# Cutting five mebibytes of zero stores into parts that load the DMA engines unevenly

## The chip, the cores and the metric

The kernel runs on one core of a Trainium2 chip. The metric is the device time of one execution in microseconds (us). Of the kernel before there are three runs, 450.79, 450.80 and 451.68 us, with a median of 450.8 us. All times and lines come from one further execution under the profiler.

## The reference

The reference is the forward pass and the gradient of a small decoder that handles one token. Two layers, A (attention) and B (a feed-forward layer), are applied twice with the same weights:

```python
x = x + A(layernorm(x)); x = x + B(layernorm(x))
x = x + A(layernorm(x)); x = x + B(layernorm(x))

# A: 32 query heads over 4 key/value heads, only the last W = 4096 of 32768 cached positions
q = x @ wq;  p = softmax(q k^T / sqrt(128));  out = (p v) @ wo
# B: h = x @ w1 + b1;  act = h * tanh(softplus(h));  out = act @ w2

out, vjp = jax.vjp(f, x, k_cache, v_cache, wq, wo, w1, b1, w2)
return out, *vjp(grad_out)
```

All is bfloat16, D = 1024, 32 x 128 = 4096 attention columns, F = 3584. The gradients of the two caches have the caches' own size, 4 x 32768 x 128 each. The positions outside of the window of 4096 get no gradient, so 28672 of 32768 rows of each head are zeros, which the kernel must write: 7 MiB for each of 8 (cache, head) pairs, 56 MiB in all. The weights' gradients are outer products of rank 2 (one row from each application of the layer), some 30 MiB, and the windows of the caches' gradients are 8 MiB.

## The kernel before, in words

The order of all work is written out by hand; nothing is rescheduled. A forward part (two A and two B layers) is followed by a backward part in reverse order, and that by a tail which forms the outer products on TensorE, evacuates them with VectorE and ScalarE (`evac`, L306 and L309) and stores them.

**Loads.** SyncE (SP in the profile) issues the weights as 1 MiB pieces into a ring of 8 slots (`Ring`, issue at L71). A piece is asked for in a fixed order and issued once a slot is free. SP issues the stores of the tail too (L1025 and L1030). Each DMA counts on one of a few semaphores that are used in turn, so an issue also waits until the DMA that used the semaphore before has landed.

**Zeros.** `zt` is a tile of 128 partitions x 4096 columns of zeros, 8 KiB per partition. The 56 MiB of zeros are cut into 56 pieces (`zjobs`), each of 128 rows of 8 KiB. GpSimd (POOL) issues them: `zeros(n, after)` at L257 first copies one element of `after` into a scratch tile (L260), which makes Pool wait until `after` has been computed, and then issues n pieces (L265). The calls are strewn over the second half of the kernel at places chosen by hand. Eight semaphores serve these DMAs in turn. The first piece is issued at 114.7 us and the last at 334.7 us of the span.

**The place of the change.** It lies at the start of the backward pass of the second B layer. `dh1` is the gradient at the activation's input, made from `da1` and the activation's derivative `mp1` (L975), and `zeros(8, dh1)` (L977) follows on Pool's queue. Then comes `dn_b1` (L836), which transposes W1 block by block on TensorE (L474), evacuates the blocks and multiplies them with `dh1` (L493), with no load in it since W1 is resident. Its result `g3` gates `zeros(4, g3)` (L981). `attn_bwd` follows, whose weights come through the ring again.

**Around the end.** `dn1` calls `twins` (L1041), which issues four copies of two rows each that spread the outer products' factors over other partitions (L1043); `take_back` (L819) issues copies of two times 8, 28 or 32 rows of 256 B for the same purpose, `rowize` (L1015) and `rowize_f` (L861) copies of 7 to 32 rows. With them ready, `unit_dw` (L1051) and `units_kv` (L1102) fill one 128 x 1024 block after another. The stores' buffers are the ring's slots, the places of the K and V windows and of W1.

Of the kernel before, what the change touches and what calls it, by code (L numbers as in the profile page):

```python
# [15 lines left out]
P = 128  # L16
# [5 lines left out]
G = 4  # L22
# [71 lines left out]
def kernel(  # L94
# [22 lines left out]
    nc = tc.nc  # L117
# [13 lines left out]
    def sb(shape, dtype, name):  # L131
        return keep.tile(shape, dtype, name=name)
# [24 lines left out]
    ZC = 4096  # L157
    zt = sb([P, ZC], BF16, "zt")
# [36 lines left out]
    for hi in range(4):  # L195
        r = slice(32 * hi, 32 * hi + 32)
# [46 lines left out]
            ring.want(("2", k, c), w2_v[:, c], [P, 4, D], own)  # L243


    zjobs = []
    for out_t in (out_2, out_3):
        for g in range(G):
            dst = out_t[0, g, 0:ZR, :].rearrange("(p r) d -> p (r d)", p=P).rearrange("p (r c) -> p r c", c=ZC)
            for k in range(dst.shape[1]):  # L250
                zjobs.append(dst[:, k, :])
    zjobs.reverse()

# [3 lines left out]
    def zeros(n, after=None):  # L257

        if after is not None and zjobs:
            nc.gpsimd.tensor_copy(pz[0:1, pz_n[0] % 16:pz_n[0] % 16 + 1], after[0:1, 0:1])  # L260
            pz_n[0] += 1
        for _ in range(n):
            if zjobs:
                dst = zjobs.pop()
                nc.gpsimd.dma_start(dst, zt[:])  # L265


    KEEP_Q = (5, 6, 7)
# [519 lines left out]
    def last_da(k):  # L788

        for c in (5, 6):  # L790
            if k == 0:
                da_dots(c)
            else:
                ring.release(("2", 0, c))
        if k:
            nc.gpsimd.memset(zt[:], 0.0)
            zeros(1)

    def wo_hook1(c):
        if c == 0:  # L800
            zeros(7, OC[:, 0, 1:2])
        if c:
            conv(1)
# [18 lines left out]
    put_by("OC", OC, HQ)  # L822
    put_by("NA", NA, TD)
    zeros(8, x3)
    sB1 = mlp_fwd(1, x3, st3, lambda: conv(1, "A"))
    put_by("NB", NB, TD)
# [4 lines left out]
    dh1 = sb([P, TF], FP32, "dh1")  # L831
# [4 lines left out]
    def dn_b1(g):  # L836

        bcast(lambda c: DHC[:, c, 1:2], STAY)
        mv_open()
        even()  # L840
        for t in range(TD):
            rowdot(W1[:, t, 0:STAY * P], [LB[0][:, 0:512]], 512, dnp[:, t:t + 1], True)
            for k in range(3):
                f0, n = STAY + 8 * k, 8
                w = W1[:, t, f0 * P:(f0 + n) * P]
                turned(w, n, lambda w=w, f0=f0, n=n, t=t, k=k: mv(w, n, TP[:, t:t + 1], lambda i: DHC[:, f0 + i, 1:2], k == 2),
                       None, f_block)
        flush()
        conv(3, "A")
        return ln_bwd(dnp, sB1["n32"], sB1["rstd"], g, "B1", lambda k: conv(k, "A"))  # L850
# [123 lines left out]

    nc.vector.tensor_tensor(out=dh1[:], in0=da1[:, 0:TF], in1=mp1[:], op=ALU.mult)  # L975
    nc.vector.tensor_copy(DHC[:, :, 1], dh1[:])
    zeros(8, dh1)  # L977
    g3 = dn_b1(g4)
    sB1["act_late"]()
    put_by("AC", AC, TF)  # L980
# [272 lines left out]
```

## Time and profile before

| | before |
|---|---|
| runs, median of 3 | 450.8 us (450.79 to 451.68) |
| profiled execution | 450.36 us, span 448.6 us |
| bytes moved by DMA | 181.40 MB, of it 58.72 MB on Pool's queue (zeros) and 121.84 MB on SP's |
| HBM | 81.84 MB read, 98.62 MB written |
| TensorE busy | 313.9 us (70%), granted clock 0.673 |
| VectorE busy | 261.2 us (58%) |
| ScalarE busy | 210.0 us (47%) |
| GpSimd busy | 38.9 us (9%), of it 29.7 us in 56 issues of zeros, 0.53 us each |
| zero piece, issue to landing | 8.5 us least, 20.5 median, 41.1 most |

How to read it: the span is the time from the first to the last instruction, and the run's time has some 1.8 us more around it. The DMA share in windows is the mean over the core's sixteen DMA engines, so one engine alone counts as 0.06; a share of 1.01 to 1.02 means that records overlap a little and that all sixteen are busy. A DMA of 128 rows is spread over the sixteen engines with 8 rows each, and it has landed when all sixteen have reported. The chain of work is followed back from the last instruction, each step to what released it.

### The profile page before, as it was taken

What the parts mean: (1) busy time and instruction counts of PE and PEld (TensorE: products, weight loads), DVE (VectorE), ACT (ScalarE), POOL (GpSimd) and SP (SyncE); (2) the same over time, 40 slices, a digit from 0 to 9 for tenths busy, and PEclk for the clock granted to TensorE, in tenths of its full rate; (3) what the DMA queues carried; (4) which work ended last, traced back from release to release, by engine and by line L of the source; (5) the groups of instructions that cost most, each with busy time, mean ns of one, the idle gap of its engine ahead of it and who ended that gap; (6) DMA issues with size and microseconds to landing.
All of it is one profiled execution on the core that took longest, in us unless ns stands there. A gap on an engine that the chain in (4) does not pass through costs nothing.

```text
span 448.6 us, 12825 instructions
## 1 busy us (share of the span) xinstructions
PE 313.9 (70%) x5681; PEld 239.7 (53%) x5681; DVE 261.2 (58%) x516; ACT 210.0 (47%) x242; POOL 38.9 (9%) x86
## 2 busy tenths in 40 slices
PE   3845542465699797986988666797966988899600
PEld 3735532455586686986986545787941222235300
DVE  4504746367551664864477447663566999998600
ACT  2501101011058576870474441570647999999600
POOL 1000000001222212102101001012130000000000
PEclk9955555556559899995798657986765555555555
DMA  8999999979999999999999999999999999999993
GB/s 336 420 420 418 421 420 418 418 312 427 393 421 422 422 420 415 398 420 423 424 423 422 427 423 419 424 393 422 424 406 415 400 417 419 417 421 408 377 408 143
DMA packets 28085, 181.40 MB, mean 404 GB/s; under 512 B 3674, under 2 KB 3702, under 8 KB 9590
## 3 DMA queue, kind: packets, MB, share of 16 engines
q1 hardware_dynamic: 19874, 121.84, 66.1%
q0 software_dynamic: 8064, 58.72, 31.5%
q8 instruction: 44, 0.72, 0.6%
q14 instruction: 11, 0.09, 0.1%
q10 hardware_dynamic: 92, 0.02, 0.0%
HBM read 81.84 MB, written 98.62 MB: 402 GB/s over the span
## 4 chain that ended last, share of the span: by engine, by line
DMA 53%; PE 22%; ACT 7%; DVE 7%; issue 4%; SPq 1%; ACTq 0%; DVEq 0%
DMA ring<-in_B_w_dram 13%; DMA W<-in_A_wo_dram 8%; PE BIG L474 8%; DMA ring<-in_A_wq_dram 7%; DMA ring<-in_A_wo_dram 5%; DMA W<-in_A_wq_dram 5%; ACT ring L309 4%; DMA out_dram<-W 4%; DMA W<-in_B_w_dram 4%; PE TP L493 3%; DMA W<-dr_AC 2%; DMA W<-in_A_k_cache_dram 2%; PE wide L1051 2%; DVE KT L306 2%; PE SC L347 2%
## 5 line engine op out<-in xcount | busy, mean ns | idle before, releaser
L309 ACT COPY ring<-BIG 128x1024 bf16<-128x1024 bf16 x52 | 51.5, 1014 | 49.3 <-PE BIG L474 45.0
L1051 PE MATMUL wide<-W 2*128 2x512 bf16 x232 | 51.7, 597 | 10.7 <-ACT ring L309 1.7
L474 PE MATMUL BIG<-ident_bf,ring 128*128 128x128 bf16 x672 | 54.3, 233 | 1.8 <-issue 1.0
L474 PEld LDWEIGHTS <-ring 128*128 128x128 bf16 x768 | 52.0, 108 | 3.4 <-issue 2.6
L451 DVE CUSTOM_DVE_ANT_0 junk<-ring,SC 128x1024 bf16<-128x1024 bf16 x32 | 38.9, 1215 | 11.6 <-DMA ring<-in_B_w_dram 11.2
L1051 PEld LDWEIGHTS <-W 2*128 2x128 bf16 x240 | 12.6, 102 | 48.1 <-issue 43.7
L493 PEld LDWEIGHTS <-ring 128*128 128x128 bf16 x864 | 29.9, 98 | 10.0 <-issue 5.8
L309 ACT CAST ring<-wide 128x1024 bf16<-128x1024 f32 x35 | 33.9, 1040 | 2.0 <-PE wide L1051 0.9
L265 POOL DMA_DIRECT2D out_dram<-zt x56 | 29.7, 534 | 50.3 <-DMA out_dram<-zt 49.3
L306 DVE CAST ring<-wide 128x1024 bf16<-128x1024 f32 (+1 forms) x29 | 32.3, 1145 | 2.5 <-PE wide L1102 1.2
L309 ACT COPY KT<-BIG 128x1024 bf16<-128x1024 bf16 x22 | 21.6, 1007 | 21.4 <-PE BIG L652 19.5
L451 DVE CUSTOM_DVE_ANT_0 junk<-ring,DSX 128x1024 bf16<-128x1024 bf16 x24 | 29.4, 1224 | 0.8
L306 DVE COPY ring<-BIG 128x1024 bf16<-128x1024 bf16 x32 | 21.8, 689 | 12.8 <-PE BIG L474 10.2
L474 PE MATMUL BIG<-ident_bf,W 128*128 128x128 bf16 x280 | 23.8, 235 | 3.4 <-DMA W<-in_A_wo_dram 2.5
L309 ACT COPY W<-BIG 128x1024 bf16<-128x1024 bf16 x20 | 20.0, 1015 | 10.0 <-PE BIG L474 9.8
L536 PE MATMUL MV<-NA,ring 128*128 128x1 bf16 x512 | 15.3, 165 | 13.2 <-DMA ring<-in_A_wq_dram 11.7
L536 PEld LDWEIGHTS <-ring 128*128 128x128 bf16 x512 | 14.7, 104 | 14.0 <-DMA ring<-in_A_wq_dram 12.5
L474 PEld LDWEIGHTS <-W 128*128 128x128 bf16 x288 | 19.3, 115 | 4.0 <-DMA W<-in_A_wo_dram 2.6
L1102 PE MATMUL wide<-W 32*128 32x256 bf16 x128 | 20.0, 403 | 0.9 <-ACT ring L309 0.6
L347 PE MATMUL YR<-ring,AC 128*32 128x256 bf16 x208 | 11.1, 372 | 11.7 <-DMA ring<-in_B_w_dram 9.3
L309 ACT CAST KT<-wide 128x1024 bf16<-128x1024 f32 x18 | 17.7, 1064 | 3.2 <-PE wide L1051 3.0
L306 DVE CAST KT<-wide 128x1024 bf16<-128x1024 f32 (+1 forms) x14 | 15.4, 1141 | 6.3 <-PE wide L1051 6.2
(272 smaller groups left out, 521.3 us busy)
## 6 DMA issues: line engine op xcount, KB each, us to landing
out_dram<-zt POOLq DMA_DIRECT2D x56, 1024.0 KB, 20.5
ring<-in_A_wq_dram SPq DMA_DIRECT2D x24, 1024.0 KB
ring<-in_A_wo_dram SPq DMA_DIRECT2D x14, 1024.0 KB
ring<-in_B_w_dram SPq DMA_DIRECT2D x13, 1024.0 KB
W<-in_A_wo_dram SPq DMA_DIRECT2D x10, 1024.0 KB
W<-in_B_w_dram SPq DMA_DIRECT2D x8, 896.0 KB
out_dram<-ring SPq DMA_DIRECT2D x13, 512.0 KB
out_dram<-ring SPq DMA_DIRECT2D x6, 1024.0 KB
```

The costliest lines, as they stand in the source:

```text
L265: nc.gpsimd.dma_start(dst, zt[:])
L306: nc.vector.tensor_copy(dst, src)
L309: nc.scalar.copy(dst, src)
L347: nc.tensor.matmul(bank[32 * j:32 * j + 32, 0:n].rearrange("p (g a) -> p g a", a=m.shape[-1]), lhsT=vec.to_broadcast([P, 32]), rhs=m, star ...
L451: nc.vector.tensor_tensor_reduce(out=out, in0=a, in1=vec, scale=1.0, scalar=acc if i else 0.0, op0=ALU.mult, op1=ALU.add, accum_out=acc)
L474: nc.tensor.transpose(b[:, i * P:(i + 1) * P], block(w, i) if block else w[:, i * P:(i + 1) * P], ident_bf[:])
L493: nc.tensor.matmul(out, lhsT=w[:, i * P:(i + 1) * P], rhs=rhs_of(i), start=fresh[0], stop=last and i == n - 1, skip_group_check=True)
L536: nc.tensor.matmul(q_ps[:, h:h + 1], lhsT=ch[:, h * P:(h + 1) * P], rhs=NA[:, t, l:l + 1], start=(k == 0 and h == 0), stop=(k == TD - 1), ...
L1051: nc.tensor.matmul(b[:, 512 * i:512 * i + 512], lhsT=R[at:at + 2, lo:lo + P], rhs=R[at:at + 2, ro + 512 * i:ro + 512 * i + 512], start=Tru ...
L1102: nc.tensor.matmul(b[:, k * 256:(k + 1) * 256], lhsT=RT[32 * g:32 * g + 32, a, tp, :], rhs=YS[32 * g:32 * g + 32, :], start=True, stop=Tru ...
```

## The change

Five of the eight pieces at L977 are written in another way. The first four pieces of the last head of the second cache gradient are joined two by two into double pieces (`zpairs`: 128 rows of 16 KiB, read twice from the same 8 KiB of zeros). Each double piece is issued as four DMAs: 5 rows, 105 rows, 12 rows, and the last 6 rows cut into sixteen parts of 6 x 1 KiB. One single piece is issued as 2 rows, 98 rows, 16 rows, and the last 12 rows cut into sixteen parts of 12 x 512 B. The other three stay whole. The bytes are the same; which of the 56 pieces are written when shifts by a few. Pool issues 15 DMAs at this place instead of 8. On the other engines the order of instructions is the same as before.

```diff
-    zjobs = []
+    zjobs, zpairs = [], []
     for out_t in (out_2, out_3):
         for g in range(G):
             dst = out_t[0, g, 0:ZR, :].rearrange("(p r) d -> p (r d)", p=P).rearrange("p (r c) -> p r c", c=ZC)
-            for k in range(dst.shape[1]):
+            n = 4 if (out_t, g) == (out_3, G - 1) else 0
+            zpairs += [dst[:, k:k + 2, :] for k in range(0, n, 2)]
+            for k in range(n, dst.shape[1]):
                 zjobs.append(dst[:, k, :])
     zjobs.reverse()
...
+    SPARED = 4
+
+    def zeros_parts(dst, parts):
+        at, m = 0, dst.shape[1]
+        for k in parts:
+            nc.gpsimd.dma_start(dst[at:at + k], zt[at:at + k, None, :].to_broadcast([k, m, ZC]))
+            at += k
+        r, c = P - at, m * ZC // 16
+        nc.gpsimd.dma_start(dst[at:P].rearrange("a m c -> a (m c)").rearrange("a (b c) -> b a c", b=16),
+                            zt[0:16, 0:r * c].rearrange("b (a c) -> b a c", a=r))
...
     nc.vector.tensor_tensor(out=dh1[:], in0=da1[:, 0:TF], in1=mp1[:], op=ALU.mult)
     nc.vector.tensor_copy(DHC[:, :, 1], dh1[:])
-    zeros(8, dh1)
+    zeros(3, dh1)
+    for dst in zpairs:
+        zeros_parts(dst, (SPARED + 1, 105, 16 - SPARED))
+    zeros_parts(zjobs.pop()[:, None, :], (2, 98, 16))
     g3 = dn_b1(g4)
     sB1["act_late"]()
```

## The prediction

> **What bounds the kernel now.** I read the profile's page first, then the chain, then windows ever closer to the end, then the Pool queue around the change.
>
> The page's lines on DMA and on the chain:
>
> ```profile
> DMA packets 28085, 181.40 MB, mean 404 GB/s; under 512 B 3674, under 2 KB 3702, under 8 KB 9590
> q8 instruction: 44, 0.72, 0.6%
> DMA 53%; PE 22%; ACT 7%; DVE 7%; issue 4%; SPq 1%; ACTq 0%; DVEq 0%
> ```
>
> The transfers carry half of the chain, and the slices of the page have DMA at 9 tenths or more from the second to the last but one. 181.40 MB over the span is 404 GB/s. So the kernel moves bytes nearly all the time, and the question is whether all sixteen DMA engines do so to the end. Windows over the last 50 us (columns: window and its length, busy time of PE, PEld, DVE, ACT and POOL, PE clock, DMA share of 16 engines, GB/s), from two calls of that view:
>
> ```profile
> 404.00:415.00 11.00, 10.49 (x75) 5.68 (x74) 9.12 (x9) 10.32 (x12) 0.00 (x0) 0.50 1.02 413
> 415.00:426.00 11.00, 6.79 (x46) 4.02 (x43) 7.41 (x7) 6.88 (x8) 0.00 (x0) 0.50 0.94 377
> 426.00:437.00 11.00, 0.00 (x0) 0.00 (x0) 0.00 (x0) 0.00 (x0) 0.00 (x0) 0.50 1.02 406
> ```
>
> ```profile
> 439.00:440.00 1.00, 0.00 (x0) 0.00 (x0) 0.00 (x0) 0.00 (x0) 0.00 (x0) 0.50 1.00 397
> 440.00:441.00 1.00, 0.00 (x0) 0.00 (x0) 0.00 (x0) 0.00 (x0) 0.00 (x0) 0.50 0.89 356
> 441.00:442.00 1.00, 0.00 (x0) 0.00 (x0) 0.00 (x0) 0.00 (x0) 0.00 (x0) 0.50 0.12 49
> 442.00:443.00 1.00, 0.00 (x0) 0.00 (x0) 0.00 (x0) 0.00 (x0) 0.00 (x0) 0.50 0.06 25
> ...
> 446.00:447.00 1.00, 0.00 (x0) 0.00 (x0) 0.00 (x0) 0.00 (x0) 0.00 (x0) 0.50 0.07 29
> 447.00:448.60 1.60, 0.00 (x0) 0.00 (x0) 0.00 (x0) 0.00 (x0) 0.00 (x0) 0.50 0.01 3
> ```
>
> No engine computes after 426; what is left is the drain of stores. All sixteen engines work until 440, fifteen of them stop at about 441, and then the share is 0.06 = 1/16 until 447.2: **one** engine alone is 6.2 us behind, with about 0.16 MB to move, and the kernel waits for it.
>
> Where does it fall behind? The trace's landing records (sixteen per DMA) answer: of the zero pieces on Pool's queue the sixteenth landing comes 0.1 us after the fifteenth at 155, 1.9 us at 185, 5.0 us at 199 and 7.1 us at 281; of the stores that end after 420 it is 5.7 to 6.5 us. It grows in the stretch in which only zeros feed the DMA, which SP's own queue shows (it issues one 14 KB copy between 149 and 183):
>
> ```profile
> 148.80 0.30 SPq L815 DMA_DIRECT2D dr_NB<-DSX  x1
> 177.53 0.35 SPq L815 DMA_DIRECT2D dr_AC<-DSX  x1
> 183.39 7.89 SPq L71 DMA_DIRECT2D ring<-in_A_wq_dram  x4
> ```
>
> In the packet records of 158 to 175 one run of 8 KiB packets, end to start, takes 346 ns each where the others take 309. The eight pieces of `zeros(8, dh1)` are issued there:
>
> ```profile
> 156.07 0.17 POOL L260 COPY pz<-dh 1x1 f32<-1x1 f32 x1
> 158.57 0.53 POOL L265 DMA_DIRECT2D out_dram<-zt  x1 [2.33 <-DMA out_dram<-zt]
> 161.09 0.53 POOL L265 DMA_DIRECT2D out_dram<-zt  x1 [1.98 <-DMA out_dram<-zt]
> ...
> 177.28 0.53 POOL L265 DMA_DIRECT2D out_dram<-zt  x1 [2.09 <-DMA out_dram<-zt]
> ```
>
> Each issue waits until the piece eight before it has landed, so Pool is idle 2 of every 2.6 us and keeps about 8 MB queued.
>
> **The change, term by term.** The same 5 MiB of zeros is written; three pieces stay whole, two doubles and one single are cut, 15 issues instead of 8.
>
> Bytes. A whole piece gives each engine 8 rows of 8 KiB, so five give 320 KiB. If the parts of 5, 105 and 12 rows are dealt to 5, 15 and 12 consecutive engines, each part beginning where the last one stopped, then 5 rows go to engines 0 to 4, 7 rows each to 5 to 15 and 0 to 3, one row each to 4 to 15: engine 4 gets 2 rows of 16 KiB, all others 8, and the last 6 rows are cut sixteen ways (6 KiB each). The single's parts (2, 98, 16) give engines 0 and 1 two rows of 8 KiB and the others 8, plus 6 KiB. Engine 4 then has 2 x 38 + 70 = 146 KiB, engines 0 and 1 have 290, the other thirteen 338 (sum 5120 KiB).
>
> - Engine 4: 174 KiB less. At the full rate of 422 GB/s (window 140 to 155), 26.4 GB/s per engine, that is 178 KB / 26.4 = 6.7 us; at 346 ns a packet 7.5. I take 6.7: if it is the late engine, it ends at 447.2 - 6.7 = 440.5.
> - The thirteen: 18 KiB more, at full rate 0.7 us. It comes as 12 packets of 1 KiB and 12 of 512 B; the nearest packet records are row copies of 1,024 B (46 ns) and 256 B (18 ns), so 0.55 plus 0.2 to 0.55. I take 0.9, nearer to the short rows: they end at 441.9 instead of 441.0. Engines 0 and 1 gain about a microsecond and matter to nobody.
> - The dip of 415 to 426 (share 0.94) is 0.66 us of every engine. There, each store is issued when the store nine before it has landed, on the late engine too. With that engine on time between 0 and 0.7 us comes back; I take 0.3.
> - Loads between 281 and 317 land up to 7.2 us later on one engine than on the other fifteen, and the chain passes through them ("DMA W<-in_A_wq_dram" until 316.90). The outer-product work that starts at 338.6 can start some us sooner. I cost that at nothing: the share is 1.01 from 300 to 415, so the bytes hide it. Below nothing it can bring what is lost in the windows 185 to 190 (375 GB/s, 0.5 us) and 281 to 300 (406, 0.7 us).
> - Pool: seven more issues and other shapes. A whole piece costs 0.53 us; a 105-row part of two pieces has 210 rows of 8 KiB, so up to 0.9. Twelve parts cost between 4 and 11 us within some 30 us in which Pool mostly waits: hidden. Behind them in Pool's queue stand the copy after g3, four zeros, and the copy of DOC (L909, issued at 203.7 before), which is read only by the transposes of L1091 at 380; the issues may end some us later without anyone waiting. If the cover were gone, the zeros-only stretch would starve: eight outstanding parts then hold as little as 2.2 MB, 5 us of supply instead of 20. That is enough for a landing, and I cost it at 0, at worst 1 to 2 us.
>
> Sum: the end of transfers moves from 447.2 to 441.0 + 0.9 - 0.3 = 441.6, **5.6 us** sooner; no one engine is late next, all sixteen are, and only fewer bytes would help. The profiled execution took 450.36 us (span 448.6), the median of the runs is 450.8, 0.4 above it; so 444.8 for the profiled one and **445.2** for the median.
>
> [...]
>
> **Rivals.**
>
> *B, slower: the parts are dealt from engine 0 up every time.* Then 5, 105 and 12 rows lie on 0 to 4, 0 to 14 (7 each) and 0 to 11: engine 4 gets 9 rows per double, engine 15 none. Engine 4 carries 2 x 22 + 6 = 50 KiB more, 1.9 us, and if it is the late one the kernel takes 1.9 us more: 452.7. It decides as soon as the start does not move on between parts. For it: SP's two-row copies (L1043) do run on two engines only, and no row shows a second start. [...] Chance 0.11.
>
> *C, no gain: the late engine is another one.* No view names engines. For engine 4: when the late engine finished its loads, at 318 to 320, the records still hold four 256 B and two 1,024 B packets of the row copies with 8 and 7 rows, issued at 296 to 306; so it is one of those that such short copies reach. Otherwise the thirteen get 0.9 us more, the late one among them: 451.7. [...] Chance 0.07.
>
> *A2, part of the gain.* The relieved engine can fall behind anew. Zeros alone feed the DMA again from about 307 to 345; at 346 against 309 ns that costs up to 12% of 35 us, 4 us. Against it: the lag did not grow over that stretch before (7.1 at 281, 5.7 at the end). With half to all of this, or with a starved queue, 1 to 4 us remain: 446.8 to 449.8. Chance 0.14.
>
> **The numbers.** Forecast 0.68: 445.2, itself between 443.6 (all dips recovered) and 446.8. With A2 the range of 443.6 to 449.9 holds 0.8. A measurement of this kernel tells 0.2%, 0.9 us, from no change. Faster: 0.68 + 0.14 = 0.82. C lies at that limit: same 0.05, slower 0.02; with B, slower 0.13.
>
> **What would show it.** Right: the windows at the end fall from 1.0 to 0 within about 1 us near 441 to 442, with no stretch of 0.06; the sixteenth landing of zeros after 200 is less than 2 us behind the fifteenth; the dip at 415 is gone. B: the stretch of 0.06 is 2 us longer, and in the parts some engine idles. C: it is as long as before. A2: it is 2 to 4 us. Loads of 290 to 317 that land early while the end stays would show that the lag was not what the end waits for, and the forecast wrong in its first step.

## The result, and the profile after

The changed kernel takes 458.7 us (median of nine runs, 452.3 to 460.8) against 451.1 us of the kernel before on the same chip (nine runs, 450.8 to 451.7). The ratio is **1.0113, 95% interval 1.0069 to 1.0157**, formed from those runs of each kernel that lie within 1.5% of its fastest, since the changed kernel scatters ten times as widely as the one before. The forecast was 445.2 us in a range of 443.6 to 449.9: it is slower, where faster was forecast. The profiled execution took 454.34 us (span 452.5) and is set against the 450.36 us (448.6) of before. So the traces account for 4 us; where the median run loses its other 4 or so, no trace of the changed kernel shows.

The windows at the end of the changed kernel (columns as in the prediction; the last two are the DMA share of sixteen engines and GB/s):

```profile
415.00:426.00 11.00, 10.79 (x78) 5.92 (x78) 9.12 (x9) 10.20 (x12) 0.00 (x0) 0.50 1.01 407
...
449.00:450.00 1.00, 0.00 (x0) 0.00 (x0) 0.00 (x0) 0.00 (x0) 0.00 (x0) 0.50 0.99 397
450.00:451.00 1.00, 0.00 (x0) 0.00 (x0) 0.00 (x0) 0.00 (x0) 0.00 (x0) 0.50 0.38 152
451.00:452.50 1.50, 0.00 (x0) 0.00 (x0) 0.00 (x0) 0.00 (x0) 0.00 (x0) 0.50 0.01 3
```

The picture is the one that the prediction asked for: from 0.99 to nothing within about a microsecond, no stretch of 0.06, no dip at 415. Only it happens at 450.5 instead of 441.6. So nine microseconds were lost on all sixteen engines, and the windows show two places, here first in the changed kernel:

```profile
175.00:185.00 10.00, 9.53 (x139) 8.96 (x137) 4.79 (x12) 7.08 (x10) 2.20 (x4) 0.76 1.02 382
185.00:190.00 5.00, 4.53 (x111) 4.46 (x108) 4.57 (x8) 4.29 (x5) 1.11 (x2) 1.00 1.07 311
190.00:195.00 5.00, 2.38 (x38) 2.38 (x38) 1.49 (x2) 1.39 (x2) 0.69 (x2) 0.84 0.90 284
...
342.00:344.00 2.00, 0.61 (x3) 0.14 (x4) 0.00 (x0) 0.19 (x1) 0.00 (x0) 0.50 0.36 148
344.00:346.00 2.00, 1.56 (x6) 0.69 (x6) 0.39 (x2) 1.86 (x4) 0.00 (x0) 0.50 0.13 43
346.00:348.00 2.00, 1.53 (x6) 0.18 (x4) 0.62 (x3) 1.89 (x4) 1.23 (x3) 0.50 0.10 41
```

The same windows in the kernel before:

```profile
175.00:185.00 10.00, 8.98 (x175) 8.39 (x173) 6.49 (x14) 8.38 (x10) 1.95 (x5) 1.00 1.01 413
185.00:190.00 5.00, 5.00 (x119) 4.93 (x117) 4.19 (x7) 4.17 (x5) 1.06 (x2) 1.00 1.00 375
190.00:195.00 5.00, 4.28 (x101) 4.09 (x99) 3.46 (x8) 3.63 (x4) 0.00 (x0) 1.00 1.02 421
...
342.00:344.00 2.00, 1.23 (x7) 0.24 (x7) 2.00 (x3) 1.99 (x4) 0.00 (x0) 0.50 1.00 412
346.00:348.00 2.00, 1.97 (x10) 0.51 (x10) 2.00 (x3) 2.00 (x3) 0.00 (x0) 0.50 1.02 414
```

In the first place the share is 0.90 to 1.07 while the rate falls from 413, 375 and 421 GB/s to 382, 311 and 284: the engines are busy with **slow packets**. Most packets are no slower: the median of the 8 KiB zero packets at 175 to 210 is 309 ns in both kernels. The mean rises from 323 to 381 ns because a few take long: 134 of 991 take over 450 ns, up to 2.5 us, where before 31 of 1,189 did, up to 0.7 us. In the second place the share itself falls to 0.1: a **hole**, in which nearly all engines have nothing to do.

To compare kernels I count, for each stretch, the time lost: its length less its bytes at 422.5 GB/s (from the packet records). The tail is the time from the moment at which a window of 1 us moves less than 110 GB/s to the end of the last packet. All in us:

| kernel | 175–210 | 281–338 | 338–350 | 350–441 | tail | ratio to before |
|---|---|---|---|---|---|---|
| before | 0.8 | 1.2 | 0.2 | 3.2 | 6.5 | |
| after | 5.0 | 0.1 | 5.8 | 2.7 | 1.0 | 1.0113 |

The four stretches lose 5.4 us in the kernel before and 13.6 in the changed one. With the 0.7 to 1.0 us of the 18 KiB more per engine the difference of 8.2 comes to 9, and that is about by how much the fifteen engines end later (441.0 before, about 450.3 now). The tail gives 5.5 back. Net it is some 4, as the two profiled executions have it (454.34 less 450.36).

Pool's queue in the cut pieces shows that it isn't the issues (0.5 to 0.75 us each) that take the time, but waiting for the piece eight before, twice 6 to 8 us where each wait was 2 to 2.5:

```profile
186.25 0.56 POOL L278 DMA_DIRECT2D out_dram<-zt  x1 [0.19 <-issue]
193.05 0.56 POOL L278 DMA_DIRECT2D out_dram<-zt  x1 [6.25 <-DMA out_dram<-zt]
...
205.54 0.54 POOL L267 DMA_DIRECT2D out_dram<-zt  x1 [7.99 <-DMA out_dram<-zt]
```

And SP's queue around the hole, first before, then after:

```profile
328.03 4.98 SPq L1043 DMA_DIRECT2D W<-W  x4
340.31 0.37 SPq L1030 DMA_DIRECT2D out_dram<-KT  x1
```

```profile
328.38 15.32 SPq L1063 DMA_DIRECT2D W<-W  x4
350.97 1.57 SPq L1050 DMA_DIRECT2D out_dram<-KT  x2
```

The four copies of `twins` take SP 15.3 us instead of 5.0, and the first store follows 10.7 us later. The packet records say why. `take_back` copies two rows at a time, and its 256 B packets lie on two engines (each of its four copies has two landings after its issue). Before, those two engines had no zeros left at about 326; 181 of the 256 B packets went between 326 and 330, at 18 ns each. In the changed kernel zeros are queued on them nearly all the time, one zero packet of 8 KiB (0.31 us) goes between most of those of 256 B, which then start 0.32 us apart, and the last of them is gone at about 342. The fourth copy of `twins` waits for that (it is issued at 343.1), and so does the first outer product (PE's queue, first before, then after):

```profile
330.55 0.61 PE L1051 MATMUL BIG<-W 2*128 2x512 bf16 x3
```

```profile
343.19 0.61 PE L1071 MATMUL BIG<-W 2*128 2x512 bf16 x3 [10.09 <-DMA W<-W]
```

It starts 12.6 us later, after waiting for `take_back`'s last copy and the short row copies behind it (L1035), not for `twins`. The stores and the last zeros (gated on `g0`) wait for the outer products, and meanwhile the other engines run out of zeros.

### The profile page after: what moved, and what is told of

Read it like the earlier page. It is cut to its first block, busy times and chain, and to the rows that moved or that the text cites. A ratio compares the mean times of both kernels' runs of the same rounds, so it can differ in the third digit from the quotient of the medians.

```text
span 452.5 us, 12830 instructions
## 1 busy us (share of the span) xinstructions
PE 315.6 (70%) x5681; PEld 241.4 (53%) x5681; DVE 261.4 (58%) x516; ACT 209.8 (46%) x242; POOL 43.3 (10%) x93
## 4 chain that ended last, share of the span: by engine, by line
DMA 42%; PE 29%; DVE 10%; ACT 9%; issue 5%; ACTq 0%; SPq 0%; DVEq 0%
DMA ring<-in_B_w_dram 13%; DMA ring<-in_A_wq_dram 10%; DMA W<-W 8%; PE BIG L491 8%; ACT ring L326 5%; DMA W<-in_A_wo_dram 4%; DMA W<-in_B_w_dram 4%; PE BIG L669 3%; PE TP L510 3%; PE wide L1071 2%; DMA W<-in_A_k_cache_dram 2%; ACT KT L326 2%; PE wide L1122 2%; PE YR L364 2%; DVE W L323 2%
## 5 line engine op out<-in xcount | busy, mean ns | idle before, releaser
L267 POOL DMA_DIRECT2D out_dram<-zt x51 | 27.2, 536 | 43.9 <-DMA out_dram<-zt 42.7
L491 PE MATMUL BIG<-ident_bf,W 128*128 128x128 bf16 x280 | 22.8, 229 | 2.8 <-DMA W<-in_A_wo_dram 1.8
L326 ACT CAST VS<-wide 128x1024 bf16<-128x1024 f32 x18 | 17.9, 1037 | 0.7 <-PE wide L1071 0.4
```

The costliest lines, as they stand in the source:

```text
L326: nc.scalar.copy(dst, src)
L491: nc.tensor.transpose(b[:, i * P:(i + 1) * P], block(w, i) if block else w[:, i * P:(i + 1) * P], ident_bf[:])
```

## Experiments

Each expectation is quoted as it was written; the letters of the theories are explained there.

### The parts by themselves (e1)

A kernel of its own that writes zeros only, stage after stage: whole pieces, whole doubles, 105 rows in a row, 105 rows with one source row per engine, rests, and the parts of the change.

```diff
+    for k in range(7):                                   # 105 rows in a row
+        nc.gpsimd.dma_start(piece(out_2, 2, k)[0:105, 0, :], z["con"][0:105, :])
+    for k in range(7):                                   # one source row per engine, nine apart
+        nc.gpsimd.dma_start(piece(out_2, 3, k)[0:105, 0, :].rearrange("(a b) c -> a b c", b=7),
+                            z["stp"][0:127:9, None, :].to_broadcast([15, 7, ZC]))
```

> Only zero stores, in stages that wait for one another; everything else of the computation is left out, so its time says nothing and only the packet records count. In turn: 7 whole pieces of 128 rows; 3 double pieces in one DMA of 128 rows each; 7 x 105 rows of a piece with 105 source rows in a row; the same 7 x 105 rows, but each of 15 engines reads one source row, the rows nine partitions apart; 6 x the rest of 6 rows cut sixteen ways; 3 double pieces in the parts of the change. Theory S (the dealing makes several engines read neighbouring source rows at once, and they hold one another up): 8 KiB packets take 309 ns in the first two stages, over 380 on average in the third, 309 to 320 in the fourth, over 380 in the last. Rival R (rows of 16 KiB or the source read twice): the second stage is slow, the third is not. Rival T (the small packets of the rests): stages one to four at 309, only the fifth and the last slow. Rival M (loads beside them): all at 309.

Windows of its stages (busy DVE and Pool, clock, share, GB/s):

```profile
20.00:34.00 14.00, 0.00 (x0) 0.00 (x0) 1.00 1.01 414
...
56.00:74.00 18.00, 0.00 (x0) 1.52 (x3) 1.00 0.89 310
78.00:93.00 15.00, 0.00 (x0) 2.47 (x5) 1.00 0.99 388
```

Whole pieces (first line) and whole doubles run at 314 ns a packet once they are under way. The 105 rows in a row (second line) move 310 GB/s with packets of 354 to 417 ns in the mean of stretches of 4 us, where fifteen engines could move 396 (15/16 of 422); the same rows nine apart (third) move 388 GB/s with 327 to 342 ns. The change's own parts move 240 to 308 GB/s with 400 to 465 ns. The medians are 309 to 315 ns everywhere. Over 450 ns take at most 0.3% of the packets of whole pieces and doubles, 5% with rows nine apart, 16% with rows in a row and 28% in the change's parts. So the source rows matter, rows of 16 KiB do not, and the rests are slow too (340 to 357 ns for 3,072 B) but few.

### Whole doubles (e2), singles (e5), singles with source rows apart (e6), doubles only (e7)

```diff
-        zeros_parts(dst, (SPARED + 1, 105, 16 - SPARED))               # e2
-    zeros_parts(zjobs.pop()[:, None, :], (2, 98, 16))
+        nc.gpsimd.dma_start(dst, zt[:, None, :].to_broadcast([P, 2, ZC]))
+    zeros(1)
...
-            zpairs += [dst[:, k:k + 2, :] for k in range(0, n, 2)]     # e5 and e6
+            zpairs += [dst[:, k:k + 1, :] for k in range(n)]
...
-            nc.gpsimd.dma_start(dst[at:at + k], zt[at:at + k, None, :].to_broadcast([k, m, ZC]))   # e6
+            nc.gpsimd.dma_start(dst[at:at + k, 0, :].rearrange("(a b) c -> a b c", b=k // e),
+                                zt[0:s * (e - 1) + 1:s, None, :].to_broadcast([e, k // e, ZC]))
...
-    zeros_parts(zjobs.pop()[:, None, :], (2, 98, 16))                  # e7
+    zeros(1)
```

> The changed kernel with the two double pieces and the single piece stored whole, in 128 rows, at the same place and in the same order: the parts are undone, the order of pieces is kept. If the parts are what slows (theory S or T), DMA keeps 410 GB/s or more from 175 to 200, one engine is again 6 us late at the end, and the time is that of the kernel before, 450.8 to 451.7. If 16 KiB rows slow (rival R), the stretch of 175 to 200 stays at 330 to 380 GB/s, and with the late engine the time is 454 or more.

> The changed kernel with its two double pieces as four single ones, each in the parts 5, 105, 12 and a rest of 6 rows: the same bytes for every engine, rows of 8 instead of 16 KiB, 23 issues instead of 15. It is the control for the next run. Theory S: the parts still read neighbouring source rows, so some 4 us of transfer are lost between 175 and 210, with zero packets of 380 ns or more on average; 452 to 460. Rival (rows of 16 KiB are part of the slowness): the loss is 2 us or less.

> As the run before, but the zeros are read from rows nine partitions apart, one source row for each engine (seven apart for the rests); destinations, bytes and dealing are the same. Theory S: the loss between 175 and 210 falls from over 4 us to about 1, zero packets there average 330 ns or less, one engine is not late at the end, the zero queue is no deeper than before at 320, so the two-row copies are not held up and the hole of 338 to 350 is gone too: 446 to 448.5. Rival (the loss comes from something else in the parts): loss and time as in the run before. Rival on the hole (it is a matter of its own): the loss is gone, the hole of 5 us stays, 450 to 453.

> The changed kernel with the single piece whole: only the two doubles are in parts. Theory S: nearly the same loss between 175 and 210 (3.5 us), and the late engine is relieved at the end; engines 0 and 1 are not spared, so their two-row copies are held up as much or more: 453 to 460. Rival (the parts of the single make the trouble): 446 to 449.

| kernel | 175–210 | 281–338 | 338–350 | tail | 8 KiB zero packets, 175–210 | ratio |
|---|---|---|---|---|---|---|
| before | 0.8 | 1.2 | 0.2 | 6.5 | 323 ns | |
| after | 5.0 | 0.1 | 5.8 | 1.0 | 381 | 1.0113 [1.0069, 1.0157] |
| e2 | 1.1 | 0.3 | 0.2 | 6.6 | 326 | 1.0001 [0.9990, 1.0013] |
| e5 | 5.2 | 0.2 | 7.0 | 1.1 | 360 | 1.0077 [1.0047, 1.0106] |
| e6 | 3.5 | 0.3 | 6.1 | 1.1 | 321 | 1.0059 [1.0039, 1.0079] |

With the doubles whole, and the single whole too, both losses go and the tail comes back: time as before. The cutting is the cause, not the joining. e6 brings the packets back to 321 ns, but most of the loss stays in another form:

```profile
185.00:190.00 5.00, 4.95 (x116) 4.83 (x114) 3.97 (x7) 4.14 (x5) 2.29 (x5) 1.00 0.94 335
190.00:195.00 5.00, 5.00 (x116) 4.91 (x114) 4.30 (x7) 4.18 (x6) 3.15 (x6) 1.00 0.88 260
```

Here the share is below 1: eight parts of singles hold 2 MB, and engines starve. e7 settles nothing: its ten times reach from 449.4 to 462.6 us (median 454.1, ratio 1.0031 [1.0005, 1.0057]), and its trace comes from one of 460 us. Doubles with source rows nine apart (e9) were not measured.

### Two-row copies as single rows, after (e3) and before (e4)

```diff
-        nc.sync.dma_start(ROWS[base:base + 2, off:off + r.shape[1] * P].rearrange("l (n p) -> l n p", p=P), r)
+        for l in range(2):
+            nc.sync.dma_start(ROWS[base + l:base + l + 1, off:off + r.shape[1] * P].rearrange("l (n p) -> l n p", p=P),
+                              r[l:l + 1])
```

> The changed kernel with each two-row copy of take_back split into two one-row copies, which can run on up to sixteen engines instead of two. Theory H (engines 0 and 1 carry 76 rows of 256 B each and serve one 8 KiB zero packet after every one of them, so the copies of L1063 end at 345 and the tail starts 16 us late): the copies of L1063 are issued by 330, the hole of 338 to 350 (206 GB/s) closes, and 5 us come back: 449 to 450 in most runs, with the spread of 452 to 461 gone. Rival (the hole comes from zeros that ran out earlier because of the parts): hole and time stay as in the changed kernel, 452 to 460.

> The kernel before with the same split of take_back alone. Theory H: the copies of L1043 are issued some 5 to 10 us sooner than 328 to 331, the tail's first block comes sooner than 338.6, and since the late engine sets the end the time moves little: 449.5 to 451. Rival: no change at all in the start of the tail, 450.8 to 451.7.

In the changed kernel the hole falls from 5.8 to 1.8 us (the tail is 2.0) and the ratio to 1.0044 [1.0013, 1.0075], so the copies are where the hole comes from. What the split changes can be seen in the kernel before: each two-row copy of L819 has two landings after its issue, each of the two one-row copies that SP issues at 320.9 and 323.4 (L1015) has sixteen. That the two engines are 0 and 1, as the expectations name them, no record shows. But eight issues take SP 14.4 us (318.8 to 333.2) and the first store still comes at 349. In the kernel before the same edit starts the stores later, at 345.5 instead of 340.3, and the time stays (1.0009 [0.9997, 1.0020]): 2.8 us are lost at 338 to 350, and the tail shrinks to 2.7. My expectation of a sooner start was wrong; SP's issues were the limit.

### The hole without any cutting (e8, e10), and a shallower queue after (e11)

```diff
-        zeros(4, DQC[:, 0, 0:1])              # e8: 6, and only steps 6 and 7 below
+        zeros(8, DQC[:, 0, 0:1])              # e10
...
-        if t in (3, 6, 7):
-            zeros(2 if t == 3 else 1, dnp[:, t:t + 1])
```

> The kernel before, all pieces whole, with two zero pieces moved from the third step of dn1 (issued at 325) to the call before it (313): the zero queue is 2 MB deeper when the two-row copies run. Theory H: engines 0 and 1 do not run out of zeros at 326, the copies of 256 B take one 8 KiB packet of waiting each for longer, those of L1043 land after 341 instead of at 338.6, and the tail starts 3 us or more later; 451 to 454. Rival (the depth of the zero queue does not matter): 450.8 to 451.7.

> The kernel before, with all four zeros that wait for steps 3, 6 and 7 of the last normalisation's gradient (issued at 325, 330 and 331 us) issued with the four before them at 313. No part is cut and no transfer time is lost before 300. Theory Q (the two-row copies can only run fast when their two engines have no zeros queued): those engines never run dry, their 256 B packets drag on until the zeros end at 340 or so, the four copies of L1043 then take 10 us or more of SP instead of 5, the first stores start at 346 to 351 instead of 340, and the hole of the changed kernel appears in the kernel before: 4 to 6 us lost between 338 and 350; 452 to 456 us. Rival P (the hole belongs to the parts or to what they did at 175 to 210): nothing is lost there, 450 to 451.5 us.

> The changed kernel, with the two zeros of step 3 (issued at 327 us) issued two steps later with those of steps 6 and 7 (332 to 334). Theory Q: the queue of zeros runs dry between about 328 and 334, the 256 B packets are done by 333 instead of 342, the copies of L1063 land by 340 and the first stores start at 342 to 345 instead of 351; the hole at 338 to 350 falls from 5.8 to 1 to 3 us, of which up to 2 come back between 328 and 336 as idle engines; 450 to 452.5 us against 454. Rival P: the hole stays and the idle time comes on top: 455 to 457 us.

Two zeros sooner (e8) change nothing: 0.9994 [0.9984, 1.0003], 1.3 us lost at 338 to 350. All four sooner (e10) make the hole of the changed kernel in the kernel before, at full size, 5.9 us:

```profile
338.00:340.00 2.00, 0.00 (x0) 0.00 (x0) 0.00 (x0) 0.00 (x0) 0.00 (x0) 0.50 0.32 126
340.00:342.00 2.00, 1.03 (x4) 0.14 (x4) 0.00 (x0) 1.06 (x3) 0.00 (x0) 0.50 0.19 65
342.00:344.00 2.00, 1.74 (x7) 0.70 (x6) 1.01 (x5) 1.75 (x5) 0.22 (x2) 0.50 0.11 35
```

```profile
330.16 11.47 SPq L1043 DMA_DIRECT2D W<-W  x4
348.10 1.59 SPq L1030 DMA_DIRECT2D out_dram<-KT  x2
```

The mechanism is shown: zeros queued on the two engines while the two-row copies run. My price was wrong. I expected 452 to 456 us and e10 takes 1.0019 [1.0008, 1.0029], 0.9 us more. Its tail is why: 1.1 us instead of 6.5, **without anything taken from engine 4**. In the hole most engines stand idle (share 0.11 to 0.32) and the late one catches up. The hole costs the fifteen 5.7 us, and the kernel, which waited for the sixteenth anyway, 0.9.

e11 moved two zeros of the changed kernel behind the copies. They were issued while the copies were still under way (335.5, with 256 B packets until 349, in a traced run of 461 us), and 1.0074 [1.0044, 1.0104] does not tell it from the changed kernel. It settles nothing.

### Cut pieces between whole ones (e12, e13)

```diff
+    zeros(1, dh1)
+    for i, dst in enumerate(zpairs):                       # three singles
+        zeros_parts(dst, (1 if i else SPARED + 1, 120))    # e12: source rows nine apart, e13: in a row
+        zeros(1)
+    zeros(1)
```

> The kernel before, with three of the eight zero pieces cut, each between whole ones: a first part of 5 rows (1 row in the second and third), then 120 rows, which are 15 engines by 8 rows from the engine behind the first part on, then the rest of 3 or 7 rows cut sixteen ways. The 120 rows read one source row per engine, nine partitions apart. Engine 4 gets about 21 rows of 8 KiB less (170 KiB, 6.4 us at 26.4 GB/s), the others 1 more; eight outstanding pieces hold about 4 MB. Theory S: 8 KiB packets stay below 330 ns and the queue doesn't starve, so the loss between 175 and 210 us is 1 to 2 us instead of 4.95. Theory Q: with little lost there, the two-row copies find their two engines dry at 326 to 329, as in the kernel before, the first stores start at 340 to 343, and the loss between 338 and 350 is 0 to 2 us. All sixteen engines then end together at 442 to 444: 445 to 447.5 us, faster than before. Rival H (the hole at 338 to 350 belongs to having no late engine): a hole of 5 us stays, 449 to 451 us.

> The same with the source rows of the 120-row parts next to one another, as in the changed kernel. Theory S: the three parts run at about 310 instead of 400 GB/s, so 2 to 3 us are lost between 175 and 210 us beyond those of the kernel with rows nine apart; 8 KiB packets there have a mean of 335 to 360 ns. By theory Q a hole of 1 to 5 us at 338 to 350 comes with that; 447 to 452 us. If rows in a row cost nothing in this mixture, both kernels take the same time and theory S is not what the changed kernel loses.

Both are slower: e12 1.0180 [1.0157, 1.0203], e13 1.0105 [1.0075, 1.0135]. 175 to 210 loses 4.7 and 5.6 us with packets of 379 and 395 ns in the mean, although e12 reads rows nine apart and never lacks supply (share 1.0); e12 loses 3.1 us more at 210 to 281. So neighbouring rows within one part are not the whole of it. The hole is gone in both (0.7 and 0.5; 6.6 and 3.2 us are lost at 281 to 338 instead, ahead of the two-row copies' end), and with the hole gone a tail of 3.9 and 5.2 us is back, in spite of 21 rows less for one engine. In these tails the share falls in steps (0.70, 0.28, 0.19, 0.11, 0.07 in e12), so several engines are late there, not one.

### What slows a packet (e14, e18)

Two more kernels that write zeros alone. In e14 every engine is given one row of the tile to read eight times, and the distance of the sixteen rows changes from stage to stage:

```diff
+    src = z[n][start:start + step * (count - 1) + 1:step, None, :].to_broadcast([count, k, ZC])
+    nc.gpsimd.dma_start(d[first:first + count], src)       # step 8, 1, 4, then 8 and 7 in turn
```

> Zeros alone, nothing else is computed, in six stages of 7 MB one after the other: (own) every engine reads one row in its own group of eight partitions, (one) the sixteen engines read sixteen neighbouring partitions, (two) rows four partitions apart, (alt) pieces in turn with rows eight apart from 0 and seven apart from 15, (set) whole pieces with sets of 4, 1 and 11 engines between, every engine always in its own group, (mix) the pieces and parts of e12. Theory O (an engine is slow when another engine reads from its group of about eight partitions at the same time, whether for the same DMA or for another one): own 310 to 320 ns for a packet of 8 KiB, one over 600 (eight engines in a group), two 400 to 620, alt 340 to 420, set 310 to 325, mix 340 to 420. Theory S as it was (only neighbouring rows within one part are slow): own, alt, set and mix all at 310 to 330 ns. Rival D (parts on fewer than sixteen engines are slow in themselves): set and mix both over 340 ns, own and alt 315.

Windows of the first four stages:

```profile
20.00:50.00 30.00, 0.00 (x0) 0.00 (x0) 1.00 0.98 201
60.00:125.00 65.00, 0.00 (x0) 0.00 (x0) 1.00 0.97 101
135.00:160.00 25.00, 0.00 (x0) 0.00 (x0) 1.00 0.98 201
170.00:195.00 25.00, 0.00 (x0) 1.36 (x3) 1.00 0.97 260
```

Rows eight apart: 638 ns a packet. Next to one another: 1,255. Four apart from 0: 638. In the fourth stage, with both distances by turns, the median is 595 to 605 in some stretches of 4 us and 309 in others. 638 and 1,255 ns are two and four times 314, as though two and four engines had to take turns at something that certain rows of the tile share. I call that a port, as a name for this effect; no record shows what it is. "Groups of eight partitions" do not fit, by which the first stage would have been the fast one. Which other rows share a port e14 does not show, and which rows an engine reads of a whole piece no record shows.

In e18 the sixteen rows are 32, 36, ..., 92 in the first three windows below, and in the fourth they lie nine apart, as in e1. That the first set shares no port was my assumption; the first window bears it out, with 411 GB/s where whole pieces have 414 in e1.

> Zeros alone, nothing else is computed, five stages of 7 MB: (own) 16 engines by 8 rows, a port for each, (set) the sets of e17, 4, 1 and 11 engines with whole pieces between, a port for each, (sp9) the singles of e6: 5, 105 and 12 rows, nine apart, and 6 cut sixteen ways, (two) 28 pieces of 16 engines by 2 rows, a port each, (sol) parts of 5 or 1 and 120 rows, nine apart, with their rest. If ports are all there is (theory O): 309 to 320 ns for a packet of 8 KiB in every stage. If small DMAs are slow in themselves (rival D): own 309, but two and set 350 ns and more. If only the sets of e17 are slow (set over 350, two 309 to 320), it is that engines work through the same pieces at different paces; if all are at 309 to 320, e17's rest comes from what runs beside the zeros.

Windows: sixteen engines by eight rows; sets of 4, 1 and 11 engines with whole pieces between; sixteen engines by two rows; parts of 5 or 1 and 120 rows:

```profile
20.00:32.00 12.00, 0.00 (x0) 2.52 (x5) 1.00 1.01 411
36.00:50.00 14.00, 0.00 (x0) 4.42 (x9) 1.00 0.99 350
82.00:94.00 12.00, 0.00 (x0) 9.69 (x20) 1.00 1.01 393
100.00:118.00 18.00, 0.00 (x0) 8.08 (x15) 1.00 0.97 356
```

Many small pieces on all sixteen engines cost 4% (393 against 411 GB/s, and no packet over 450 ns after the first 2 us). Pieces on some of the engines cost 13 to 15%: the median stays at 309 to 331 ns, but one packet in seven (sets) or twelve (parts) takes over 450, up to 900. So a second thing slows cut pieces, with nothing beside them and, in the sets, with rows that gave 411 GB/s when all sixteen engines read them at once. What it is I don't know. In common these stages have DMAs that leave engines out, so that, as I take it, engines work at the same time on different pieces: where every DMA runs on all sixteen engines (whole pieces and doubles in e1, the first and third window here) at most 0.3% of the packets take over 450 ns, where DMAs leave engines out 5 to 28% do (in e1 and here). The records of these stages also hold packets of 4 bytes beyond the sixteen of each DMA (230 in e1, 629 in e18, 116 in the changed kernel, none in before, e2 and e16); whether they have to do with it is not shown, as the loss does not go by their number.

### A port for every engine, in the kernel (e15, e16, e17)

```diff
-                nc.gpsimd.dma_start(dst, zt[:])                                       # e16, all 56 pieces
+                nc.gpsimd.dma_start(dst.rearrange("(a b) c -> a b c", b=8),
+                                    zt[32:93:4, None, :].to_broadcast([16, 8, ZC]))
...
+        for w, a in enumerate((0, 32, 8, 40, 16, 48, 24)):     # e15: rows 8 apart; e17: e16 and rows 4 apart
+            if w % 2:
+                wave(d[:, a:a + 8], 0, 4, 8)                   # first engine, engines, rows for each
+                wave(d[:, 32 + w // 2:33 + w // 2], 4, 1, 1)
+                wave(d[:, a:a + 8], 5, 11, 8)
+            else:
+                wave(d[:, a:a + 8], 0, 16, 8)
```

e15 and e17 write three of the eight pieces in sets of 4 engines with 8 rows each, 1 engine with one row and 11 engines with 8 rows each, with a whole piece between any two sets, and the 21 rows left over cut sixteen ways at the end. In e15 engine e is given row 8e, so that by theory O every engine has a group of its own. In e16 and e17 it is given row 32 + 4e. Theory O by then said that engines which share a port slow one another, and I took these sixteen rows to share none, which e14 had not shown.

> [...] Engine 4 gets 21 rows less (172 KB, 6.5 us at 26.4 GB/s), every other 10.5 KiB more. Theory O: packets stay at 325 ns or less and 1 us or less is lost between 175 and 210; with theory Q the two-row copies then find their engines dry, as in the kernel before, 0 to 2 us are lost at 338 to 350, and all sixteen engines end together at 442 to 444: 444.5 to 447 us, faster than before. Rival D (small DMAs of Pool are slow in themselves): 3 to 5 us are lost between 175 and 210 and up to 5 behind it, 450 to 458 us.

> The kernel before, with one edit: every zero piece is read from sixteen rows of the zero tile (32, 36, ... 92) instead of 128, engine e reading row 32 + 4e eight times. [...] Theory O: 8 KiB zero packets take 309 to 316 ns on every engine, nothing more than before is lost between 175 and 210. If shared ports also make the one engine late (theory L), all sixteen end together at 441 to 443: 444 to 446.5 us, faster than before. Rival M (the late engine has more to do, the row copies, and ports have no part in it): the stretch of one engine at the end stays, 450 to 451.5 us. If sixteen rows are slower than 128 (638 ns as in e14), 500 us and more.

> e16 with the sparing of engine 4 from e15: three of eight pieces in sets of 4, 1 and 11 engines, 21 rows cut sixteen ways, every engine reading row 32 + 4e only. Theory O: e15's loss between 175 and 210 (13 us, packets 565 ns) came from rows eight apart, which share ports two by two, and goes: 0 to 1.5 us there, packets 309 to 320 ns. Rival D (small DMAs of Pool are slow in themselves): 4 us and more stay. If engine 4 is late by ports (theory L), it now ends some 6 us early and the others at 442 to 443: 444.5 to 447 us, not better than e16. If it is late by its own load (rival M), e17 takes 444.5 to 447 us where e16 stays at 450 to 451.

| kernel | 175–210 | 281–338 | 338–350 | tail | 8 KiB zero packets, 175–210 | ratio |
|---|---|---|---|---|---|---|
| e15 | 13.3 | 4.8 | 0.7 | 2.1 | 565 ns | 1.0276 [1.0253, 1.0300] |
| e16 | 1.0 | 1.2 | 0.1 | 6.4 | 324 | 1.0001 [0.9992, 1.0010] |
| e17 | 4.3 | 2.7 | 0.3 | 4.9 | 372 | 1.0040 [1.0022, 1.0058] |

e15, built on "groups of eight", reads rows eight apart, which took 638 ns in e14, and is the slowest of all; the same sets from rows 32, 36, ..., 92 (e17) lose a third of that. e16 answers another question: whole pieces from these sixteen rows run exactly as before (324 ns against 323), and the tail stays (6.4 us against 6.5). So it is not the source rows that make the one engine late. e17 takes 21 rows of 8 KiB from one engine, meant to be engine 4 (6.5 us at 26.4 GB/s), and its end is this:

```profile
446.00:447.00 1.00, 0.00 (x0) 0.00 (x0) 0.00 (x0) 0.00 (x0) 0.00 (x0) 0.50 0.31 127
447.00:448.00 1.00, 0.00 (x0) 0.00 (x0) 0.00 (x0) 0.00 (x0) 0.00 (x0) 0.50 0.19 78
448.00:449.00 1.00, 0.00 (x0) 0.00 (x0) 0.00 (x0) 0.00 (x0) 0.00 (x0) 0.50 0.06 25
...
450.00:451.00 1.00, 0.00 (x0) 0.00 (x0) 0.00 (x0) 0.00 (x0) 0.00 (x0) 0.50 0.06 25
```

The tail is 4.9 us again. Here several engines are late: five engines' worth of share at 446, three at 447, and one alone from 448 on.

### Cutting later pieces (e19)

```diff
         if t in (3, 6, 7):
-            zeros(2 if t == 3 else 1, dnp[:, t:t + 1])
+            zeros(2 if t == 3 else 0, dnp[:, t:t + 1])
+            if t > 3:
+                zeros_cut(5 if t == 6 else 1)              # 5 or 1 row, 120 rows nine apart, rest
...
-    zeros(2, g0)
+    zeros(0, g0)
+    zeros_cut(1)
+    zeros(1)
```

> The kernel before, with the eight pieces behind the activation's gradient whole as they were, and three later ones cut (those issued at 330, 331 and 334 us): 5 rows (1 in the second and third), 120 rows on the 15 engines other than 4, the rest cut sixteen ways, source rows nine apart. Engine 4 gets 21 rows of 8 KiB less (6.4 us). All loads have landed by then, and the two-row copies too in the kernel before (329). If the relief is worth what the prediction took (5.6 us) and only the place was wrong: nothing more is lost at 175 to 210 and at 338 to 350, packets of the cut pieces may cost 0.5 to 1.5 us, all engines end together at 442 to 443.5: 445 to 447.5 us, faster than before. Rival: the parts starve or slow the stretch of 333 to 345 by as much as they relieve: 449 to 453 us.

1.0148 [1.0131, 1.0165]; four of its five runs take 456 to 458 us, the traced one 452.4. In the traced one 175 to 210 loses 0.9 us as before, 338 to 350 loses 2.5, 281 to 338 loses 3.9, and the tail is 4.2 in spite of the relief. The landing records say why (see "Engine 4" below): the engine left out was not the late one.

No version beats the kernel before; e2, e4, e8 and e16 can't be told from it.

## Why the prediction was wrong, step by step

**"One engine alone is 6.2 us behind" was right**, and so was that the kernel waits for it.

**"Engine 4 … it ends at 440.5" is the step that the runs do not bear out.** The changed kernel's clean end looks like its proof, and isn't. Among kernels in which nothing is cut, the tail goes with the hole at 338 to 350: holes of 0.1 to 0.2 us leave tails of 6.4 to 6.6 (before, e2, e16), 1.3 leaves 5.3 (e8), 2.8 leaves 2.7 (e4), 5.9 leaves 1.1 (e10). A hole of 5.8 would explain a tail of 1.0 without any relief. And where 21 rows were taken from one engine and there was next to no hole, the tail was 3.9, 5.2 and 4.9 us (e12, e13, e17), instead of none.

No run shows the dealing from which engine 4's 174 KiB less were worked out (5, 15 and 12 engines, each part from where the last one stopped). What the runs show of it: 105 rows nine apart had a DMA share of 0.99 (e1), where fifteen engines, always the same, would give at most 15/16 = 0.94 by my estimate; so if a part of 105 rows leaves one engine out, it is not the same one each time.

The landing records, from which the prediction read the lag, also tell whom the relief hit, as I read them: each of Pool's 63 DMAs in the changed kernel has sixteen landings, the parts of 2 and 5 rows too, so an engine that is left out of a DMA lands it as soon as it is through with the one before. In e13 the first landing of the 120 rows comes at 175.80, 0.4 us after the first of the DMA before, too soon for eight rows of 0.31 us, and the next at 179.00, while the last engine lands the DMA before at 179.71 and its own share of the 120 rows at 183.06: it got its eight rows, and an engine that was early anyway was left out. e12 (first 175.87, next 177.79), e17 (176.47, 178.51), e19 (335.56, 337.98) and e5 (182.05, 184.71) show the same. So there the relieved engine was not the late one, and the tail of 1.1 in e5 came with a hole of 7.0 alone.

In the changed kernel it is otherwise. By 183.81 fourteen engines had landed the five rows, the last two at 185.44 and 185.97, and the first landing of the 105 rows comes at 186.18: the engine left out was one of these two. After the second double it is 5.9 us ahead of all others (187.92 against 193.85). So here the relief did reach a late engine, and hole and relief each could have made the clean end. e3, the same parts with a smaller hole, gives a size for the relief: with a hole of 1.8 its tail is 2.0, where 4.4 lies between e8 and e4 (holes of 1.3 and 2.8), so some 2.4 us by this estimate, in which the slow packets may have a share. Why the engine left out is a late one in some kernels and an early one in others, that is, with which engine the dealing begins, no run shows; no record names engines.

The prediction's sign for its success, a sixteenth landing less than 2 us behind the fifteenth after 200, does not come either: up to 285 it is 1.7 to 3.3 us in the changed kernel, and all sixteen lie 11 to 19 us apart.

**"I cost it at 0, at worst 1 to 2 us" (Pool) is the first step that failed**, by 4.2 us (5.0 lost at 175 to 210 instead of 0.8). I asked whether Pool's issues and the bytes in its queue suffice, and for the changed kernel's doubles they nearly do: the share stays near 1 until 190. What I took for granted was that a row of 8 KiB takes 309 to 346 ns whichever engine reads it from where. It took 381 in the mean, with 151 of 991 packets over 400 ns. The choice of source rows accounts for part of it (by themselves, in e1, rows in a row 310 and nine apart 388 GB/s; in the kernel 565 ns in e15 and 372 in e17), the unknown second thing for another (e18). How the 4.2 us divide between the two, the runs do not show. Where the packets were made fast, the starvation of which I had spoken came, at 3.5 us and not 1 to 2 (e6).

**"I cost that at nothing: … the bytes hide it" (the start of the tail) is the second**, by 5.6 us (5.8 lost at 338 to 350 instead of 0.2). The loads did land evenly, and 281 to 338 lost 1.1 us less, about the 0.5 and 0.7 that I gave as the bound below nothing. But the start of the outer products hangs on 256 B packets, which share two engines with the zeros. The first outer product moved from 330.6 to 343.2, and the wide blocks, whose beginning the prediction gave as 338.6, went from 336.3 to 348.9. The share of 1.01 told me that the DMA has work, and I read it as though order within an engine's queue could not matter. e10 shows the mechanism without the change. An early loss does not always make the hole (e12, e13 and e17 lost as much at 175 to 210 and have none): it comes when the zeros queued by 316 to 334 leave those two engines no gap.

**"The thirteen", 0.9 us**, fits in size: the sum of losses needs 0.7 to 1.0 to reach the measured 9. The packets are others than I assumed: the records have the rests as three packets of 4,096 B (203 ns in the mean) and three of 2,048 B (131 ns) for each engine, 1.0 us together, not as 12 of 1 KiB and 12 of 512 B. **"The dip", 0.3**: 1.1 came back between 404 and 441, more than I took, and e10 has the same gain, so it too belongs to the engine that catches up.

Rivals B and C gave 452.7 and 451.7, near what the better runs took, but by other ways: a tail longer or as long as before. B, parts dealt from engine 0 up, would have left 2 us more of it, and no kernel with parts has that. A2 named a starved queue; none of the rivals had packets slow on all engines, or the hole.

## What to carry to other kernels

When an end is set by one late DMA engine, the others' slack is as large as its lag, and anything that stalls all of them repays itself from that slack (e10: 5.7 us of stall cost 0.9): judge a cure by the time at which the many end, not by whether the tail is gone. In these runs, pieces for some of the engines slowed everybody's packets by more than they relieved one, for a reason that is not known in full; so where a DMA must be cut, cut it so that all sixteen engines keep working through the same pieces, from source rows that do not slow one another (e18: 393 GB/s so, 350 and 356 with parts for some). Short rows on few engines want a gap in the bulk traffic of those engines before them (256 B took 18 ns a packet without zeros between, and 0.32 us from one to the next with them), and a DMA share of 1.0 says nothing on whether they have it. And whether a cure reached the engine that it was meant for can be read from the order of the landings.

## What the hardware showed that I had not expected

- A packet of 8 KiB took 638 ns when the sixteen source rows lay eight apart, or four apart from 0, and 1,255 when they lay next to one another (e14), against 309 to 314 in whole pieces. Distance alone does not decide it: rows four apart from 0 moved 201 GB/s (e14), four apart from 32 moved 411 (e18).
- Sixteen source rows (32, 36, ..., 92), one for each engine, served 56 MiB of zeros as well as 128 rows (e16, 1.0001).
- With two queues on one engine, a zero packet of 8 KiB and a packet of 256 B went mostly by turns, 0.32 us for the two: 76 rows of 256 B on each of two engines took from 320 to about 342 us, against 18 ns a packet once the zeros' queue was dry.
- Parts for some of the engines, with nothing else running, moved 350 to 356 GB/s where whole pieces moved 411, with single packets up to 0.9 us (e18); 28 pieces on all sixteen engines moved 393.
- The kernels with cut pieces scatter: 452.3 to 460.8 us for the changed one against 450.8 to 451.7 before.
